# Chunk attention followed by a GELU MLP: GpSimd's casts of later tiles in pieces of 256 elements

## The chip, the cores and the metric

The kernel runs on one core of one Trainium2 chip. Its metric is the device time of one execution in microseconds, as the median over several runs. Besides the times there is one execution taken by the hardware profiler; the profile and the trace that are read below are of that execution. A core has five engines, each with its own queue of instructions: TensorE (PE, with its weight loads shown as PEld), VectorE (DVE), ScalarE (ACT), GpSimd (POOL) and SyncE (SP), which here issues nearly all DMAs. Engines wait for each other through semaphores.

## The reference

```python
def _attn_ref(q, k, v):                       # each (8, 8, 576, 64): batch, heads, sequence, head size
    chunk = 64; nc = S // chunk               # nine chunks of 64 rows
    q_c, k_c, v_c = (a.reshape(B, H, nc, chunk, D) for a in (q, k, v))
    scores = scale * np.matmul(q_c, k_c.transpose(0, 1, 2, 4, 3))
    scores = scores - np.max(scores, axis=-1, keepdims=True)
    attn = np.exp(scores)
    attn = attn / (np.sum(attn, axis=-1, keepdims=True) + 1e-09)
    return np.matmul(attn, v_c).reshape(B, H, S, D)

def _moe_ref(x, w_in, w_out):                 # x (4608, 512), w_in (512, 2048), w_out (2048, 512)
    h = x @ w_in
    g = 0.5 * h * (1.0 + erf(h / sqrt(2)))
    return g @ w_out
```

Attention acts within chunks of 64 rows; its output, with the heads side by side, is the input of a two-layer MLP with the exact GELU.

## The kernel before, in words

**Tiles.** The 4608 rows are worked in nine tiles of 512, numbered 0 to 8. Tiles 0 to 7 are eight chunks of one batch each; tile 8 gathers the ninth chunk of every batch. A tile goes through attention (scores, exponential, sums, product with V) and through the two matmuls of the MLP. While TensorE works on the MLP of tile t, the attention of tile t + 1 and the loads of tiles t + 2 and t + 3 are woven in.

**Saved products.** From tile 1 on both matmuls of the MLP are done in blocks with seven products in place of eight. That takes sums and differences of blocks, which VectorE forms: `x_sums` (line 557) from the attention output, `g_sum` (lines 657 and 670) from the hidden values, `w_in_sums` and `weight_sum` (lines 551 and 522) from the weights. All of these are bf16 subtractions or additions with both inputs in SBUF. The intermediate results of the products are joined by `plus` (line 578), which adds a bank of PSUM and a tile in SBUF and writes either the bank or the tile; TensorE's next product into that bank, at line 574, waits for it. ScalarE copies banks (lines 588 and 591) and applies the GELU (line 582).

**Inputs.** Queries, keys and values arrive as float32 in staging tiles (`arrival`, six of them). `load_qk` (lines 106 to 128) issues one DMA for the queries of a tile and four for its keys, one for each 128 rows; `load_v_rows` issues nine for V of a tile, four for the even heads and five for the odd ones, and sixteen for tile 8. Casts to bf16 follow: `cast_qk` (lines 164 to 171), once for each of four pairs of heads (queries) or of four groups of 128 rows (keys), 512 elements in each partition; and `cast_v_rows` (lines 206 to 210), once for the even and once for the odd heads, 1024 elements each. The function that they are given as `copy` says which engine does it: `PO` is GpSimd, `DV` is VectorE, `AC` is ScalarE. For tiles 2 and later the casts are GpSimd's, but for the keys of tile 2, which VectorE casts. Then `flip` (lines 198 to 204) turns the bf16 queries and keys by a DMA transpose from SyncE's queue, which SyncE issues when the casts are done; `quad_S` multiplies them, and `quad_av` (line 321) reads the cast V as it is.

**Order.** The order of all work is written out by hand. `STEPS` (tiles 2 to 4) and `WHOLE` (tiles 4 to 8) are lists of step names: `CQ`, `CK` and `CV` are the casts of queries, keys and V, `LQ`, `LK`, `LV` the loads, `FQ` and `FK` the flips, `XS1` to `XS4` the `x_sums`, `S1a` to `S4b` the `g_sum`s, `s12` and `c22+` the additions at line 578. In tiles 5 and later the loads and casts stand in `next_loads` (lines 1149 to 1157). Each engine takes its own instructions in this order and waits at an instruction until what it needs is there. `K0` is 2 and `T0` is 3.

Of the kernel before, what the change touches and what calls it, by code (L numbers as in the profile page):

```python
# [11 lines left out]
def kernel(  # L12
# [18 lines left out]
    J = 4  # L31
    PC = CH // J
    G = H // 2
# [3 lines left out]
    CT = NC - 1  # L37
# [126 lines left out]
    def cast_qk(t, nm, g, copy):  # L164
        st = tiles[t]
        if nm not in st:
            st[nm] = ld.tile([P, G, J, 2, D], bf16, tag="k", name="k_nat", bufs=3)
        if nm == "k" and t >= K0:
            copy(st[nm][:, :, g], st[nm + "f"][:, :, g].rearrange("p (q r) d -> p q r d", r=2))  # L169
            return  # L170
        copy(st[nm][:, g].rearrange("p j r d -> p r j d"), st[nm + "f"][:, 2 * g:2 * g + 2])  # L171

# [33 lines left out]
    def cast_v_rows(t, copy):  # L206
        st = tiles[t]
        st["v"] = ld.tile([P, H, CT // 2, D], bf16, tag="v", name="v_nat")
        for r in range(2):
            copy(st["v"][:, r::2], st["vf"][:, r::2])  # L210

    AT, TP, MM = (ps_at, "at"), (ps_tp, "tp"), (ps_mm, "mm")
    ALONE, BETWEEN = (AT, AT, AT, TP), (MM, MM, AT, AT)
# [255 lines left out]
    T0 = 3  # L469
# [181 lines left out]
    def g_sum(t, i, part=None):  # L651

        st = tiles[t]
        n = HF // 2
        if i == 3:
            st["S", 3] = [s3_sb[:, 0:n], s3_sb[:, n:HF]]
            nc.vector.tensor_tensor(s3_sb[:], g_block(t, 0, 0), g_block(t, 1, 0), op=SUB)
            return
        if ("S", i) not in st:
            if i == 4:  # L660
                st["S", i] = [work.tile([P, n, HD], bf16, tag="t1", name="s4", bufs=2)[:] for _ in range(2)]
            else:
                st["S", i] = [flat(k_bds[2 * (i - 1) + a], n) for a in range(2)]
        f = slice(n * part, n * (part + 1))
        a, b, op = {1: (g_block(t, 1, 0), g_block(t, 1, 1), ADD),
                    2: (None, g_block(t, 0, 0), SUB),
                    4: (g_block(t, 0, 1), None, SUB)}[i]
        a = st["S", 1][part] if a is None else a[:, f]
        b = st["S", 2][part] if b is None else b[:, f]
        nc.vector.tensor_tensor(st["S", i][part], a, b, op=op)  # L670
# [113 lines left out]
    def play(t, order):  # L784
# [23 lines left out]
        for m in range(G):  # L808
            does[f"E{m}"] = lambda m=m: quad_exp(n, m)
            does[f"E+{m}"] = lambda m=m: quad_exp(n + 1, m)  # L810
            does[f"ov{m}"] = lambda m=m: quad_over(n, m)
            if t <= T0:
                does[f"R{m}"] = lambda m=m: att_rc(n, m)
                does[f"X{m}"] = lambda m=m: quad_x_plain(n, m)
            else:
                does[f"R{m}"] = lambda m=m: quad_rc(n, m // 2, m % 2)
                does[f"X{m}"] = lambda m=m: quad_x(n, m // 2, m % 2)
            does[f"P{m}"] = lambda m=m: quad_part(n + 1, m // 2, m % 2)
            does[f"XS{m + 1}"] = lambda m=m: x_sums(n, (m,))
            does[f"xs{m + 1}"] = lambda m=m: x_sums(t, (m,))  # L820
            for of in range(4):
                does[f"W{of}.{m}"] = lambda m=m, of=of: w_in_sums(of, (m,))
            does[f"CQ{m}"] = lambda m=m: cast_qk(t + 3, "q", m, PO)
            does[f"CK{m}"] = lambda m=m: cast_qk(t + 3, "k", m, PO)
        does["LQ"], does["LK"] = lambda: load_qk(t + 3, "q"), lambda: load_qk(t + 3, "k")
        does["FQ"], does["FK"] = lambda: flip(n + 1, "q"), lambda: flip(n + 1, "k")
        does["LV"], does["CV"] = lambda: load_v_rows(n + 1), lambda: cast_v_rows(n + 1, PO)
        does["Q8"] = lambda: [load_qk(NT - 1, "q"), pool_cast_qk(NT - 1, "q")]
        for step in order:
# [96 lines left out]
    def pool_cast_qk(t, names="qk"):  # L926
        for nm in names:
            for g in range(G):
                cast_qk(t, nm, g, PO)
# [33 lines left out]
    with tc.manual_schedule():  # L963
# [62 lines left out]
        for c in range(1, NWC):  # L1026
# [8 lines left out]
            if c < 3:  # L1035
                r = slice(CH * (c - 1), CH * c)
# [85 lines left out]
        for t in range(1, NT):  # L1122
            n = t + 1
# [7 lines left out]
            if t == 1:  # L1131
                mm1_slices(1, {0: mm, 1: at, 2: at, 3: mm, 8: mm},
                           (((0, 1, 2), (0,)), last_av, ((0, 1, 2), (1,)), ((3,), (0, 1)), ((8,), (0, 1)),
                            ((0, 1, 2, 3, 8), (2,)), ((0, 3, 8, 1, 2), (3,))))
                x_sums(1)
                for g in range(G):
                    cast_qk(2, "k", g, DV)
                flip(2, "q")
                load_v_rows(2, (0,))
                flip(2, "k")  # L1140
                for ms, y_sb in held:
                    store(0, ms, y_sb)
                held.clear()
                load_v_rows(2, (1,))
                cast_v_rows(2, PO)
                bring_qk(3)
            if t > T0 and n + 1 < NT:
                flip_qk(n + 1)
            def next_loads():
                if t + 3 == NT - 1:  # L1150
                    load_qk(t + 3, "k")
                    pool_cast_qk(t + 3, "k")
                elif t + 3 < NT:
                    bring_qk(t + 3)
                if n + 1 < NT:
                    load_v_rows(n + 1)
                    cast_v_rows(n + 1, PO)
# [7 lines left out]
            g = [[lambda i=i, a=a: g_sum(t, i, a) for i in (1, 2, 4)] for a in range(2)]  # L1165
# [61 lines left out]
```

## Time and profile before

| what | value |
|---|---|
| time, median of 3 runs | 267.56 us (267.51 to 269.14) |
| the profiled execution's own time | 267.8 us |
| its span (first to last instruction) | 266.0 us |
| TensorE clock granted | 1.00 |
| ScalarE busy | 190.7 us, 72% |
| VectorE busy | 223.3 us, 84% |
| GpSimd casts of V, 128x1024 | 14, 1116 ns mean |
| GpSimd casts of keys, 128x512 (line 169) | 24, 671 ns mean |
| GpSimd casts of queries, 128x512 (line 171) | 31, 672 ns mean |
| HBM read and written | 36.70 MB and 9.44 MB |

How to read it: an engine's busy time is the union of its instructions; waiting, branching and the issue of DMAs are not counted. "L574" is line 574 of the kernel. `out<-in` are the program's own tile names, followed by partitions x elements and the type. In the chain of work that ended last, each row is a start, a length and what the time went to; "issue" there is time in which the engine waited for nothing that the profile shows. In a row of the timeline the start and length come first, "x4" is four merged instructions, and square brackets give the engine's idle time before it and what ended that. The ends of matmuls are modelled, so two starts, not one length, tell TensorE's pace. The 31 query casts at line 171 are those of tiles 1 to 8, of which tiles 4 to 8 have 20.

### The profile page before, as it was taken

How to read it: one execution, taken by the hardware profiler on the slowest of the kernel's cores; microseconds unless marked ns; L12 is line 12 of the kernel's file. 1: busy time of each engine (PE TensorE's matmuls, PEld its weight loads, DVE VectorE, ACT ScalarE, POOL GpSimd, SP SyncE). 2: the span in 40 equal slices, each digit the busy share in tenths (PEclk: the TensorE clock that was granted, in tenths of full speed). 3: DMA queues.
4: the chain of work that ended last, by engine and by line, in shares of the span. 5: the costliest groups of instructions: out<-in, count | busy, mean ns of one | idle time of the engine just before them, and what ended most of it. 6: DMA issues, size and time to landing. Idle time of an engine off the chain costs nothing.

```text
span 266.0 us, 7735 instructions
## 1 busy us (share of the span) xinstructions
PE 256.3 (96%) x3121; PEld 210.7 (79%) x3121; DVE 223.3 (84%) x383; ACT 190.7 (72%) x386; POOL 86.1 (32%) x142
## 2 busy tenths in 40 slices
PE   7799999999999999999999998999999999999994
PEld 2478875556888888887878887888888888888883
DVE  6875977989897679678999999999999999947853
ACT  3767758988758988898887587948794789227820
POOL 7768778701267030730540371213200300000000
PEclk9999999999999999999999999999999999999999
DMA  6999998999898989999999988978874220121014
GB/s 209 270 341 402 392 403 210 278 217 276 226 267 206 208 225 276 261 255 234 262 248 193 292 198 215 206 158 192 245 164 90 93 81 2 41 81 41 2 39 118
DMA packets 123412, 53.98 MB, mean 203 GB/s; under 512 B 97776, under 2 KB 120304, under 8 KB 123376
## 3 DMA queue, kind: packets, MB, share of 16 engines
q1 hardware_dynamic: 123072, 53.23, 78.2%
q8 instruction: 24, 0.39, 0.6%
q10 hardware_dynamic: 304, 0.26, 0.3%
q14 instruction: 12, 0.10, 0.1%
HBM read 36.70 MB, written 9.44 MB: 173 GB/s over the span
## 4 chain that ended last, share of the span: by engine, by line
PE 70%; SPq 9%; DMA 6%; ACT 6%; DVE 5%; issue 2%; DVEq 0%
PE hs_ps L574 26%; PE y_ps L734 19%; PE y_ps L764 11%; DMA arrival<-in_moe_w_in_dram 3%; ACT h L582 3%; PE h_ps L438 3%; PE y_ps L897 3%; SPq L123 3%; SPq L162 2%; DMA arrival<-in_k_dram 2%; SPq L117 2%; PE h_ps L454 2%; PE av_ps L321 1%; PE y_ps L861 1%; PE h_ps L464 1%
## 5 line engine op out<-in xcount | busy, mean ns | idle before, releaser
L582 ACT ACTIVATE h<-hs_ps 128x512 bf16<-128x512 f32 x87 | 49.6, 609 | 7.3 <-PE hs_ps L574 6.4
L574 PEld LDWEIGHTS <-w_in_sb 128*128 128x128 bf16 x348 | 33.9, 98 | 4.6 <-issue 0.2
L171 POOL CAST q_nat<-arrival 128x512 bf16<-128x512 f32 x31 | 19.6, 672 | 51.1 <-DMA arrival<-in_q_dram 31.2
L210 POOL CAST v_nat<-arrival 128x1024 bf16<-128x1024 f32 x14 | 15.6, 1116 | 54.0 <-DMA arrival<-in_v_dram 33.5
L574 PE MATMUL hs_ps<-x,w_in_sb 128*128 128x256 bf16 x232 | 31.8, 272 | 0.0
L734 PEld LDWEIGHTS <-h 128*128 128x128 bf16 x240 | 23.2, 98 | 2.8
L961 ACT ACT_TABLE_LOAD x16 | 20.5, 1283 | 1.0 <-PEq L1211 0.7
L694 ACT COPY kept<-y_ps 128x512 f32<-128x512 f32 (+1 forms) x17 | 9.0, 537 | 16.1 <-PE y_ps L734 13.1
L734 PE MATMUL y_ps<-w_out_sb,h 128*128 128x256 bf16 x160 | 18.6, 273 | 0.0
L734 PE MATMUL y_ps<-v_bd,k_bd 128*128 128x256 bf16 x160 | 18.5, 273 | 0.1
L169 POOL CAST k_nat<-arrival 128x512 bf16<-128x512 f32 x24 | 15.4, 671 | 8.2 <-DMA arrival<-in_k_dram 8.1
L734 PEld LDWEIGHTS <-k_bd 128*128 128x128 bf16 x160 | 15.6, 98 | 2.1 <-issue 0.2
L591 ACT COPY hs_ps<-hs_ps 128x512 f32<-128x512 f32 x29 | 16.2, 582 | 0.6 <-PE hs_ps L574 0.5
L574 PE MATMUL hs_ps<-k_bd,w_in_sb 128*128 128x256 bf16 x116 | 16.6, 272 | 0.0
L466 ACT ACTIVATE h<-h_ps 128x512 bf16<-128x512 f32 x21 | 12.5, 605 | 5.3 <-PE h_ps L438 3.9
L244 ACT ACTIVATE pT<-s_ps 128x512 bf16<-128x512 f32 x28 | 14.4, 599 | 1.8 <-PE s_ps L236 1.8
L764 PEld LDWEIGHTS <-h 128*128 128x128 bf16 x144 | 13.8, 98 | 1.7
L699 DVE TENSOR_TENSOR kept<-y_ps,kept 128x512 f32<-128x512 f32 (+1 forms) x16 | 10.4, 649 | 5.4 <-issue 4.0
L574 PE MATMUL hs_ps<-k_bd,w_in_more 128*128 128x256 bf16 x96 | 14.2, 273 | 0.2 <-DVE hs_ps L578 0.2
L574 PEld LDWEIGHTS <-w_in_more 128*128 128x128 bf16 x128 | 12.5, 98 | 2.4 <-issue 0.7
L438 PE MATMUL h_ps<-x,w_in_sb 128*128 128x256 bf16 x128 | 14.3, 273 | 0.1
L438 PEld LDWEIGHTS <-w_in_sb 128*128 128x128 bf16 x128 | 12.3, 98 | 1.9 <-DVE w_in_sb L942 0.4
(158 smaller groups left out, 632.0 us busy)
## 6 DMA issues: line engine op xcount, KB each, us to landing
arrival<-in_v_dram SPq DMA_DIRECT2D x58, 128.0 KB, 3.0
arrival<-in_k_dram SPq DMA_DIRECT2D x28, 256.0 KB, 5.8
arrival<-in_q_dram SPq DMA_DIRECT2D x7, 1024.0 KB, 6.5
out_dram<-kept SPq DMA_DIRECT2D x24, 256.0 KB, 2.8
arrival<-in_moe_w_out_dram SPq DMA_DIRECT2D x4, 1024.0 KB, 12.0
arrival<-in_moe_w_in_dram SPq DMA_DIRECT2D x6, 512.0 KB, 7.9
out_dram<-y_sb SPq DMA_DIRECT2D x8, 256.0 KB, 3.0
arrival<-in_v_dram SPq DMA_DIRECT2D x28, 64.0 KB, 2.6
```

The costliest lines, as they stand in the source:

```text
L169: copy(st[nm][:, :, g], st[nm + "f"][:, :, g].rearrange("p (q r) d -> p q r d", r=2))
L171: copy(st[nm][:, g].rearrange("p j r d -> p r j d"), st[nm + "f"][:, 2 * g:2 * g + 2])
L210: copy(st["v"][:, r::2], st["vf"][:, r::2])
L244: nc.scalar.activation(pT[:].rearrange("p u (c j) -> p u c j", j=J), tiles[t]["s_ps"][m // 2][m % 2][:].rearrange("p u (j c) -> p u c j", ...
L438: nc.tensor.matmul(to[:, cols], left, right[:, cols], start=(start and a == 0), stop=stop, skip_group_check=True)
L466: nc.scalar.activation(tiles[t]["h"][:, f, :], h_ps[:], Act.Gelu)
L574: nc.tensor.matmul(hs[:, f], left[:, ks, f * P:(f + 1) * P], right[:, ks], start=(fresh and f == 0 and ks == 0), stop=(ks == 1), skip_grou ...
L582: nc.scalar.activation(h[:, n:n + HM, HD * c:HD * (c + 1)], src, Act.Gelu)
L591: "s11": lambda: AC(place_of("b")[:], bank["a"][:]),
L734: nc.tensor.matmul(to, left(f, m), right[:, f], start=(fresh and (split or m == 0) and f == 0), stop=(f == HF - 1), skip_group_check=True)
L764: nc.tensor.matmul(bank[name][:, m], left(f, m), right[:, f], start=(fresh and m == 0 and f == 0), stop=(f == HF - 1), skip_group_check=True)
L961: nc.scalar.activation(act_scratch[:], rest[:, 0:1], func)
```

## The change

Three loops are added around copies. Keys of tile 2 and later (the condition is `t >= K0`) are cast in two pieces of two pairs of heads each. Queries of tiles after 3 (`t > T0`) are cast in two pieces, each with two of the four positions `j`. V is cast in four pieces for each half of the heads, one for every 128 rows, wherever `cast_v_rows` is called, which is for tiles 2 to 8. Each piece has 256 elements in each partition where the copy had 512 or 1024. The engine of each cast stays, so the keys of tile 2 are cast in pieces on VectorE. No load, no flip and no other step is moved.

```diff
@@ -166,7 +166,12 @@
         if nm not in st:
             st[nm] = ld.tile([P, G, J, 2, D], bf16, tag="k", name="k_nat", bufs=3)
         if nm == "k" and t >= K0:
-            copy(st[nm][:, :, g], st[nm + "f"][:, :, g].rearrange("p (q r) d -> p q r d", r=2))
+            for q0 in range(0, G, 2):
+                copy(st[nm][:, q0:q0 + 2, g], st[nm + "f"][:, 2 * q0:2 * q0 + 4, g].rearrange("p (q r) d -> p q r d", r=2))
+            return
+        if t > T0:
+            for j in range(0, J, 2):
+                copy(st[nm][:, g, j:j + 2].rearrange("p j r d -> p r j d"), st[nm + "f"][:, 2 * g:2 * g + 2, j:j + 2])
             return
         copy(st[nm][:, g].rearrange("p j r d -> p r j d"), st[nm + "f"][:, 2 * g:2 * g + 2])
@@ -207,7 +212,8 @@
         st = tiles[t]
         st["v"] = ld.tile([P, H, CT // 2, D], bf16, tag="v", name="v_nat")
         for r in range(2):
-            copy(st["v"][:, r::2], st["vf"][:, r::2])
+            for n in range(CT // 2):
+                copy(st["v"][:, r::2, n], st["vf"][:, r::2, n])
```

## The prediction

> **What bounds the kernel now.** I read the page first (busy times, then the chain that ended last), then TensorE's waits after 75 us, then the timeline at the places where TensorE waits. From the page:
>
> ```profile
> span 266.0 us, 7735 instructions
> ...
> PE 256.3 (96%) x3121; PEld 210.7 (79%) x3121; DVE 223.3 (84%) x383; ACT 190.7 (72%) x386; POOL 86.1 (32%) x142
> ...
> PE 70%; SPq 9%; DMA 6%; ACT 6%; DVE 5%; issue 2%; DVEq 0%
> ```
>
> TensorE carries the chain; GpSimd, whose casts are edited, is busy a third of the span and has no share in the chain. So the casts can matter only through something that reaches TensorE. After 75 us TensorE's waits are one line:
>
> ```profile
> PE hs_ps L574 <- DVE hs_ps L578: 1.4, 3, 0.7
> ```
>
> Three waits, all for VectorE's addition at L578. The chain shows them from its own side:
>
> ```profile
> 85.97 0.62 DVE hs_ps L578
> 86.63 4.09 PE hs_ps L574 x36
> ...
> 137.68 0.60 ACT kept_p L588
> 138.27 0.69 DVE hs_ps L578
> ...
> 147.92 0.64 PE av_ps L321 x64
> ...
> 163.37 0.46 issue
> 163.83 0.70 DVE hs_ps L578
> 164.57 8.46 PE hs_ps L574 x76
> ...
> 250.22 12.24 PE y_ps L734 x112
> ```
>
> The last row gives TensorE's pace: 12.24 us over 112 matmuls, 0.109 us each. From 164.57 on it never waits for another engine. Whatever the change saves or costs must pass through three places: near 86, 139 and 164 us.
>
> Why VectorE is late there is seen in the timeline of the first place:
>
> ```profile
> 81.72 2.67 POOL L171 CAST q_nat<-arrival 128x512 bf16<-128x512 f32 x4 [3.77 <-DMA arrival<-in_q_dram]
> ...
> 82.15 0.46 DVE L551 TENSOR_TENSOR arrival<-w_in_sb 128x512 bf16<-128x512 bf16 x1
> ...
> 82.53 0.82 DVE L551 TENSOR_TENSOR arrival<-arrival,w_in_sb 128x512 bf16<-128x512 bf16 x1
> ...
> 83.28 0.68 DVE L578 TENSOR_TENSOR hs_ps<-hs_ps,kept_p 128x512 f32<-128x512 f32 x1
> ...
> 83.88 0.78 DVE L557 TENSOR_TENSOR k_bd<-x,k_bd 128x512 bf16<-128x512 bf16 x1
> ...
> 85.19 0.78 DVE L551 TENSOR_TENSOR arrival<-w_in_sb,arrival 128x512 bf16<-128x512 bf16 x1
> ...
> 85.80 0.60 PE L574 MATMUL hs_ps<-k_bd,w_in_sb 128*128 128x256 bf16 x4
> ```
>
> and of the other two:
>
> ```profile
> 135.93 1.07 POOL L210 CAST v_nat<-arrival 128x1024 bf16<-128x1024 f32 x1 [1.75 <-PE hs_ps L574]
> 136.01 1.26 DVE L557 TENSOR_TENSOR k_bd<-x 128x512 bf16<-128x512 bf16 x1
> ...
> 137.66 0.69 DVE L262 TENSOR_REDUCE part<-pt 128x16 f32<-128x512 bf16 x1
> ...
> 137.91 0.60 PE L574 MATMUL hs_ps<-k_bd,w_in_more 128*128 128x256 bf16 x4
> ```
>
> ```profile
> 151.32 1.10 DVE L670 TENSOR_TENSOR s<-h,k_bd 128x1024 bf16<-128x1024 bf16 x1
> ```
>
> ```profile
> 155.36 0.87 DVE L670 TENSOR_TENSOR s<-h,k_bd 128x1024 bf16<-128x1024 bf16 x1
> 156.16 0.82 DVE L557 TENSOR_TENSOR k_bd<-x 128x512 bf16<-128x512 bf16 x1
> ...
> 157.51 0.41 DVE L557 TENSOR_TENSOR k_bd<-x 128x512 bf16<-128x512 bf16 x1
> ...
> 161.99 0.85 DVE L557 TENSOR_TENSOR k_bd<-x,k_bd 128x512 bf16<-128x512 bf16 x1
> ...
> 163.23 0.69 DVE L262 TENSOR_REDUCE part<-pt 128x16 f32<-128x512 bf16 x1
> ```
>
> ```profile
> 162.81 1.04 PE L574 MATMUL hs_ps<-x,w_in_sb 128*128 128x256 bf16 x8
> ```
>
> The reader is to see one shape with two durations. A bf16 subtraction of 512 elements with both inputs in SBUF takes 0.41 us at 157.51, and 0.78 to 1.26 where it starts inside a GpSimd cast: at 136.01 it starts 0.08 us into the V cast and ends 0.27 after it, so it ran only when the cast let go. The L578 addition, which reads one input from PSUM, takes 0.68 inside casts at 83.28 and 0.70 at 163.83: it isn't held. For the 1024-element form:
>
> ```profile
> L670 DVE TENSOR_TENSOR k_bd<-k_bd,h x16: 679/684/693, 63.3 to 252.7; 128x1024 bf16<-128x1024 bf16 x16
> ```
>
> so 0.68 undisturbed against 1.10 and 0.87 above. VectorE's losses against these bases are: first place 0.05 + 0.41 + 0.37 + 0.37 = 1.20 us; 0.85 ahead of the second; 0.42 + 0.19 + 0.41 + 0.44 = 1.46 between 151 and 163. At the third they cannot drain away, because VectorE has next to no idle time:
>
> ```profile
> 140.00:160.00 20.00, 20.00 (x300) 17.60 (x298) 19.73 (x37) 14.53 (x27) 6.84 (x9) 1.00 1.05 222
> ```
>
> (VectorE 19.73 of 20 us; the last columns are clock, DMA share and GB/s.)
>
> **The change part by part.** *GpSimd's own cost.* No 128x256 cast is in the trace. Its neighbours:
>
> ```profile
> 73.24 2.29 POOL L171 CAST q_nat<-arrival 128x512 bf16<-128x512 f32 x4 [3.26 <-DMA arrival<-in_q_dram]
> ```
>
> ```profile
> 133.56 0.62 POOL L169 CAST k_nat<-arrival 128x512 bf16<-128x512 f32 x1 [0.31 <-DMA arrival<-in_k_dram]
> ```
>
> ```profile
> 138.26 1.04 POOL L210 CAST v_nat<-arrival 128x1024 bf16<-128x1024 f32 x1 [1.27 <-DMA arrival<-in_v_dram]
> 138.69 3.10 SPq L204 DMA_TRANSPOSE q_t<-q_nat  x1
> ```
>
> ```profile
> L176 POOL CAST v_bd<-arrival 64x256 bf16<-64x256 f32 x26 | 10.4, 401 | 1.4
> ```
>
> 512 elements take 0.62, 1024 take 1.04: 0.42 per 512, so 256 take 0.62 - 0.21 = 0.41; the 64x256 row's 0.40 agrees. Four in a row take 2.29, so the next starts (2.29 - 0.62) / 3 = 0.56 after the last, 0.06 before its end; for 256 that spacing is 0.35, for 1024 0.98. Bounds: 0.28 (half of 0.56, no fixed part) and 0.56 (all of it fixed); I take 0.35. By the diff, V of seven tiles goes from 14 casts to 56, keys of tiles 3 to 8 from 24 to 48, queries of tiles 4 to 8 from 20 to 40. GpSimd gains 14 x (1.40 - 0.98) + 44 x (0.70 - 0.56) = 12 us (bounds 2 and 42), some 2 us per tile, against 180 idle us.
>
> *What hides it.* Keys and queries are next read by the flips on SyncE's queue. For tile 6 the last key cast ends at 134.18 and the flip is issued at 138.69: 4.5 us of cover. The last cast starts when its DMA lands and becomes two pieces, 0.14 later; even the eight casts' whole growth, 8 x 0.14 = 1.1, is covered (at the upper bound 8 x 0.56 = 4.5 uses up the cover, and what exceeds it stands in front of SyncE's next loads). V's last cast of tile 5 ends at 139.30 and is read by the attention matmuls at 147.92. Each V piece reads only the rows that one load of the sequence brings, so pieces start as loads land; the last piece ends some 0.6 earlier than now (1.04 - 0.41). No load is brought forward by that: the DMA share is already 1.05.
>
> *VectorE's own casts.* Keys of tile 2 go through the same branch, on VectorE: four casts become eight.
>
> ```profile
> 55.96 0.43 DVE L169 CAST k_nat<-arrival 128x512 bf16<-128x512 f32 x1 [0.22 <-DMA arrival<-in_k_dram]
> ...
> 59.36 0.70 DVE L578 TENSOR_TENSOR hs_ps<-hs_ps,kept_p 128x512 f32<-128x512 f32 x1 [0.70 <-PE hs_ps L574]
> ```
>
> The last waits for its DMA, so only that one's growth counts: between 0 and another 0.43, I take 0.15. It lies under the 0.70 that VectorE then waits for TensorE. Zero on the path.
>
> *VectorE's losses.* A held VectorE instruction waits for the rest of one cast. With pieces the longest rest falls from 0.56 to 0.35 for queries and keys (x 0.63) and from 0.98 to 0.35 for V (x 0.36). First place, all q and k: 1.20 to 0.75, 0.45 saved. Third: (0.42 + 0.19 + 0.41) x 0.63 + 0.44 x 0.36 = 0.80, 0.66 saved.
>
> What of it reaches TensorE: first place, four matmuls from 85.80 last 0.44 at pace, so the next was due at 86.24 and began at 86.63: 0.39 lost, of which 0.45 saved would cover all; I take 0.35, since the new pieces are met at other moments. Second: due 137.91 + 0.44 = 138.35, began 139.00, 0.65 lost; but the chain comes here from ScalarE's copy ending at 138.28 and the 0.69 of L578 follows it. VectorE's own lateness (L262 ends at 138.35) is worth at most 0.1; I take 0.05. Third: due 162.81 + 0.87 = 163.68, began 164.57, 0.89 lost. L578 could have started at 163.37, where the chain shows 0.46 of "issue" under the reduce before it; those 0.46 fall to the 0.66 saved, the rest is the instruction's own time. What is late next there is L578 itself. Sum: 0.35 + 0.05 + 0.46 = 0.86 us.
>
> A rule speaks against the mechanism. The trace first: the casts at 73.24 overlap by 0.06, yet the VectorE instruction at 82.53 ran in between two of the four queued casts. The Trainium skill, "GPSIMD Engine Reference", section "Instruction dispatch", says that consecutive Pool instructions are no barrier, that each of its cores goes on to the next when its own share is done; if so the port need not fall free between two pieces. The same skill's "SBUF — State Buffer", section "Who interferes with whom", has the port held for one whole instruction and then given up. By the first there would be no saving, by the second the 0.86 stands; 82.53 agrees with the second.
>
> **The rivals.** *A: the gain stays hidden.* VectorE is let in earlier, but TensorE's three waits are set by what L578 adds to (second place shows it). Saving 0 to 0.3: 267.3 to 267.6. For: the 138.27 row. Against: "issue" at 163.37.
>
> *B: VectorE loses more.* If a waiting instruction lets more than one piece by, the loss follows GpSimd's total port time instead of one piece's length. It decides from 0.56 / 0.35 = 1.6 pieces per wait on. Port time goes from 14 x 0.98 + 44 x 0.56 = 38.4 to 144 x 0.35 = 50.4, x 1.31. The first place then loses another 0.37, the third 1.46 x 0.31 = 0.45 and, where the 0.85 at 136.01 has not drained, 0.26 more: +1.1 us, 268.6; at the 0.56 bound (80.6, x 2.1) 1.3 + 1.6 + 0.9 = +3.8, 271.4. For: the overlap at 73.24. Against: 82.53 and 155.36, where one cast is let by. The page's rule on Pool instructions is this rival.
>
> *C: more than the sum.* All losses vanish and the three waits go altogether: 0.39 + 0.65 + 0.89 = 1.93, 265.6. It is the ceiling of this mechanism.
>
> *D: the flips are late.* Only near the 0.56 bound; then SyncE's loads slip by a us or so per tile while DMA is full: 269 to 270.
>
> **How the numbers follow.** The profiled execution took 267.8 us, 1.8 beyond its span and 0.24 above the median of 267.56. 267.8 - 0.86 = 266.9 for it; for the median 266.7. Chances: forecast (266.4 to 267.2) 0.55; A 0.18; B 0.13; C 0.08; D and what I don't see 0.06. A measurement of this kernel can tell about 1%, 2.7 us, from no change. Faster by that would need 264.9, beyond the ceiling C: 0.05, for an effect not seen here. Slower by it, over 270.2, needs B near its bound, or D: 0.11. The range leaves out half of C below and the worse half of B and D above: 265.6 to 269.0.
>
> **What would show it.** In the profile after: 128x256 casts of about 0.41 us; L557 and L670 instructions no longer than about 0.41 and 0.68 plus 0.35; the waits of TensorE for L578 at about 0.9 us or less in place of 1.4; flips still issued well after their casts. Forecast wrong: L557 instructions again over 1 us (B), shorter ones with TensorE's waits unchanged (A), casts of over 0.6 us (D), or a new wait of TensorE on another line.

## The result, and the profile after

| | before | after |
|---|---|---|
| median, 20 runs each | 268.08 us (266.61 to 269.55) | 266.69 us (265.30 to 268.05) |
| ratio of the times | 1 | 0.9944, 95% interval 0.9926 to 0.9961 |
| profiled execution, its span | 267.8, 266.0 us | 268.05, 266.3 us |

The change makes the kernel about 1.4 us faster: 0.56%, with an interval that excludes no change. That lies inside the 1% which the prediction called no change, and inside its range; the forecast was 0.86 us, so the sign was right and the size too small. (The median of before has moved from 267.56 with the 17 runs added.)

One thing has to be said before the profile is read: of the 20 executions of after, the profiled one was the slowest, and that of before lay below its median. The two spans don't show the gain. Both kernels were therefore profiled again, before once and after twice (experiments 8 to 10).

The page of after, first execution; in the last three rows the two numbers behind the bar are busy us and mean ns of one:

```profile
PE 256.8 (96%) x3115; PEld 211.8 (80%) x3121; DVE 222.3 (84%) x387; ACT 190.3 (71%) x386; POOL 103.6 (39%) x228
...
PE 76%; ACT 14%; DVE 4%; DMA 3%; issue 1%; POOL 0%; SPq 0%; ACTq 0%; POOLq 0%
...
L216 POOL CAST v_nat<-arrival 128x256 bf16<-128x256 f32 x56 | 24.6, 463 | 38.6 <-DMA arrival<-in_v_dram 38.2
...
L174 POOL CAST q_nat<-arrival 128x256 bf16<-128x256 f32 x40 | 17.6, 488 | 48.3 <-DMA arrival<-in_q_dram 48.3
...
L170 POOL CAST k_nat<-arrival 128x256 bf16<-128x256 f32 x48 | 19.1, 442 | 3.6 <-DMA arrival<-in_k_dram 3.6
```

The pieces are there in the forecast numbers: 56, 40 and 48. GpSimd is busy 17.5 us longer (103.6 against 86.1) and its share of the chain is 0%.

Line numbers behind the casts have grown by 6, so L578 is now L584, L574 is L580, L557 is L563 and L670 is L676. TensorE's waits after 75 us, in the waits view of after (line, what it waited for: us in total, times, longest), in the first and then in the third execution:

```profile
PE y_ps L770 <- ACT kept L777: 0.8, 1, 0.8
PE s_ps L242 <- DMA k_t<-k_nat: 0.6, 1, 0.6
PE hs_ps L580 <- DVE hs_ps L584: 0.2, 1, 0.2
```

```profile
PE y_ps L770 <- ACT kept L777: 0.5, 1, 0.5
PE hs_ps L580 <- DVE hs_ps L584: 0.2, 1, 0.2
```

In the second execution, whose span is 263.7 us, the same view has no row at all. Of the three waits for L578, 1.4 us, there remains one of 0.2 or none. In the first and third executions something else stands in their place, a wait of 0.5 to 0.8 us for `kept` at L777, and in the first also one for the flip of the keys. (Neither needs the pieces: see experiments 8 to 10.) In the chain of the first execution:

```profile
79.00 5.69 PE hs_ps L580 x52
...
96.61 3.59 DMA out_dram<-kept
...
100.27 0.59 ACT kept L777
...
102.81 0.64 PE av_ps L327 x64
...
161.17 12.23 PE hs_ps L580 x112
...
250.49 12.24 PE y_ps L740 x112
```

At the first place TensorE now runs through: 52 matmuls in 5.69 us, 0.109 each. At the third it runs through as well, 112 in 12.23. But at 100.27 ScalarE had to wait for an output DMA of 3.59 us before it could fill `kept` again. The wait for the flip, at 93 us, is one of TensorE that isn't on this chain.

What is nearly the same in every execution of one kernel is the time from the 64 attention matmuls near 101 us to the last 112 matmuls. Here 250.49 - 102.81 = 147.68 us. Before, in its two profiled executions (the last 112 matmuls of the first, at 250.22, are in the prediction):

```profile
101.24 0.64 PE av_ps L321 x64
```

```profile
102.50 0.64 PE av_ps L321 x64
...
251.76 12.24 PE y_ps L734 x112
```

That is 148.98 and 149.26. After, second and third execution:

```profile
100.40 0.64 PE av_ps L327 x64
...
247.93 12.24 PE y_ps L740 x112
```

```profile
101.51 0.64 PE av_ps L327 x64
...
249.24 12.24 PE y_ps L740 x112
```

147.53 and 147.73. In this stretch, which holds the second and third place, the change saves 1.25 to 1.7 us in every pair of executions. Ahead of it the kernels differ by as much between two executions of one kernel (101.24 and 102.50; 100.40 to 102.81) as from each other, and that is where the slow first profile of after lost what it had gained.

VectorE's subtractions, grouped by shape in before and in after (shortest/median/longest ns, from and to us):

```profile
L670 DVE TENSOR_TENSOR k_bd<-h x16: 647/684/1258, 62.5 to 251.9; 128x1024 bf16<-128x1024 bf16 x16
...
L557 DVE TENSOR_TENSOR k_bd<-x x14: 381/417/1275, 78.1 to 235.5; 128x512 bf16<-128x512 bf16 x14
L557 DVE TENSOR_TENSOR k_bd<-x,k_bd x14: 410/415/852, 78.5 to 236.9; 128x512 bf16<-128x512 bf16 x14
```

```profile
L676 DVE TENSOR_TENSOR k_bd<-h x16: 648/688/906, 62.9 to 252.2; 128x1024 bf16<-128x1024 bf16 x16
...
L563 DVE TENSOR_TENSOR k_bd<-x x14: 382/419/699, 78.5 to 235.8; 128x512 bf16<-128x512 bf16 x14
L563 DVE TENSOR_TENSOR k_bd<-x,k_bd x14: 415/476/619, 79.2 to 237.2; 128x512 bf16<-128x512 bf16 x14
```

The last of the three numbers tells the story: the longest waits go from 0.86 us (1275 - 417) to 0.28 (699 - 419). Counted over the trace from 60 us on, with 0.41, 0.68 and 1.22 us as the undisturbed lengths for 512, 1024 and 2048 elements and waits of some 0.05 us and more, VectorE lost 6.6 us in 15 waits before and 3.3, 3.9 and 5.3 us in 20, 24 and 30 waits in the three executions after. A wait now costs 0.16 to 0.18 us on average in place of 0.44, and there are more of them.

### The profile page after: what moved, and what is told of

Its sections match the earlier page's. It is cut to its first block, busy times and chain, and to the rows that moved or that the text cites. A ratio compares the mean times of both kernels' runs of the same rounds, so it can differ in the third digit from the quotient of the medians.

```text
span 266.3 us, 7808 instructions
## 1 busy us (share of the span) xinstructions
PE 256.8 (96%) x3115; PEld 211.8 (80%) x3121; DVE 222.3 (84%) x387; ACT 190.3 (71%) x386; POOL 103.6 (39%) x228
## 3 DMA queue, kind: packets, MB, share of 16 engines
q1 hardware_dynamic: 123072, 53.23, 78.9%
## 4 chain that ended last, share of the span: by engine, by line
PE 76%; ACT 14%; DVE 4%; DMA 3%; issue 1%; POOL 0%; SPq 0%; ACTq 0%; POOLq 0%
PE hs_ps L580 25%; PE y_ps L740 22%; PE y_ps L770 9%; ACT h L588 5%; PE h_ps L444 5%; PE y_ps L903 3%; ACT pT L250 2%; PE av_ps L327 2%; ACT L967 1%; DMA out_dram<-kept 1%; PE y_ps L867 1%; PE h_ps L460 1%; DMA arrival<-in_k_dram 1%; PE tp L187 1%; ACT k_bd L200 1%
## 5 line engine op out<-in xcount | busy, mean ns | idle before, releaser
L216 POOL CAST v_nat<-arrival 128x256 bf16<-128x256 f32 x56 | 24.6, 463 | 38.6 <-DMA arrival<-in_v_dram 38.2
L580 PEld LDWEIGHTS <-w_in_sb 128*128 128x128 bf16 x348 | 33.9, 98 | 4.7 <-issue 0.2
L174 POOL CAST q_nat<-arrival 128x256 bf16<-128x256 f32 x40 | 17.6, 488 | 48.3 <-DMA arrival<-in_q_dram 48.3
L580 PE MATMUL hs_ps<-x,w_in_sb 128*128 128x256 bf16 x232 | 31.8, 272 | 0.0
L170 POOL CAST k_nat<-arrival 128x256 bf16<-128x256 f32 x48 | 19.1, 442 | 3.6 <-DMA arrival<-in_k_dram 3.6
L580 PE MATMUL hs_ps<-k_bd,w_in_sb 128*128 128x256 bf16 x116 | 16.6, 272 | 0.0
L580 PEld LDWEIGHTS <-w_in_more 128*128 128x128 bf16 x128 | 12.5, 98 | 2.3 <-issue 0.5
L580 PE MATMUL hs_ps<-k_bd,w_in_more 128*128 128x256 bf16 x96 | 14.2, 273 | 0.0
```

The source lines that it names most:

```text
L170: copy(st[nm][:, q0:q0 + 2, g], st[nm + "f"][:, 2 * q0:2 * q0 + 4, g].rearrange("p (q r) d -> p q r d", r=2))
L174: copy(st[nm][:, g, j:j + 2].rearrange("p j r d -> p r j d"), st[nm + "f"][:, 2 * g:2 * g + 2, j:j + 2])
L216: copy(st["v"][:, r::2, n], st["vf"][:, r::2, n])
L580: nc.tensor.matmul(hs[:, f], left[:, ks, f * P:(f + 1) * P], right[:, ks], start=(fresh and f == 0 and ks == 0), stop=(ks == 1), skip_grou ...
```

## The experiments

All edits are to the changed kernel unless it is said otherwise; ratios are to the kernel before, on the same chip, with a 95% interval. "Stretch" is the time from the attention matmuls near 101 us to the last 112 matmuls, read from the chain as above.

**1 and 2. One half of the change alone.** First V alone, with the casts of queries and keys as they were; then queries and keys alone, with V as it was.

```diff
-            for q0 in range(0, G, 2):
-                copy(st[nm][:, q0:q0 + 2, g], st[nm + "f"][:, 2 * q0:2 * q0 + 4, g].rearrange("p (q r) d -> p q r d", r=2))
+            copy(st[nm][:, :, g], st[nm + "f"][:, :, g].rearrange("p (q r) d -> p q r d", r=2))
             return
-        if t > T0:
-            for j in range(0, J, 2):
...
```

> V alone in pieces of 256, queries and keys whole as before. Theory (a VectorE subtraction with two SBUF inputs waits for the rest of one GpSimd cast, so the length of a cast is what counts): of TensorE's three waits the first (0.39 us, all queries and keys) stays, the second (0.65) loses about 0.3, the third (0.89) loses about 0.3; 0.6 us less than before, ratio about 0.998. Rival (what helps is that V pieces start as their loads land, a shift in time): all of the change's gain is here, ratio about 0.9945. In the trace the theory expects subtractions of up to 0.8 us beside query and key casts and none over 0.8 beside V casts.

```diff
-            for n in range(CT // 2):
-                copy(st["v"][:, r::2, n], st["vf"][:, r::2, n])
+            copy(st["v"][:, r::2], st["vf"][:, r::2])
```

> Queries and keys alone in pieces of 256, V whole as before. Theory (length of a cast): the first wait goes (0.39), the third shrinks by about 0.4, the second stays; 0.8 us less than before, ratio about 0.997. Rival (V pieces that start with their loads): ratio about 1.000. The theory expects subtractions of 1.2 us beside V casts to remain and those beside query and key casts to stay under 0.65 (512 elements).

V alone: 267.86 us, 0.9972 (0.9940 to 1.0004). Queries and keys alone: 267.31 us, 0.9945 (0.9920 to 0.9970). The gain of queries and keys is clear of no change. For V alone the interval reaches 1 and also holds the rival's 0.9945, so the time decides nothing about V; nor is it shown which half gives more, since the two intervals overlap. The two gains, 0.28% and 0.55%, sum to 0.83%, which the intervals don't tell from 0.56%. VectorE's waits split as they should: beside whole V casts a subtraction of 512 elements still took 1.26 us (0.85 lost), beside pieces of V none lost more than 0.21 us. So did TensorE's losses at the three places, by start times: with V alone 0.28, 0.35 and 0.59 us (in an execution that was the slowest of its twelve), with queries and keys alone none at the first and the third, and 1.16 at the second. The stretch is 149.0 us with V alone and 148.5 with queries and keys alone.

The trace of queries and keys alone held a surprise. Timeline, start and length first:

```profile
132.20 1.80 POOL L170 CAST k_nat<-arrival 128x256 bf16<-128x256 f32 x5
132.51 1.76 DVE L562 TENSOR_TENSOR k_bd<-x,k_bd 128x512 bf16<-128x512 bf16 x1
```

```profile
PE hs_ps L579 <- DVE hs_ps L583: 1.0, 1, 1.0
```

A subtraction of 0.41 us took 1.76. Of the five key pieces in this row, which follow each other without a gap, four lie wholly within it, and TensorE then waited 1.0 us at the second place. This is rival B's mechanism, seen for the first time; it happened to one of 17 held instructions of this execution. Of the 74 in the three executions of the changed kernel none lost more than 0.29 us, less than the 0.345 us from one queued piece to the next.

**3 and 4. Is it the length of a piece, or its earlier start?** A V piece of the change reads only the rows of one load (of two for the last odd piece and in tile 8), so it can start as soon as these have landed; that alone could spread the casts out. Here V is cut by heads instead: pieces of 256 elements again, but each reads all loads of its half of the heads, four or five (in tile 8 eight), so none starts before the last one.

```diff
-            for n in range(CT // 2):
-                copy(st["v"][:, r::2, n], st["vf"][:, r::2, n])
+            for h in range(r, H, 2):
+                copy(st["v"][:, h], st["vf"][:, h])
```

> Queries and keys in pieces as in the change; V in four pieces for each half too, but one for each head, so that every piece needs all loads of its half and none starts early. The pieces are as short (256 elements). Theory (length): the same gain as the change, ratio 0.993 to 0.996. Rival (V pieces that start with their loads): the gain of V is gone, ratio as with queries and keys alone, 0.997 to 1.000.

> V in four pieces by heads, queries and keys as in the change, again. Theory (only the length of a piece counts): the same as the change within 0.002. Its first ratio, 0.991 [0.988, 0.9941], left open that it is better; if that was real it is 0.99 to 0.992 here too and beats the change by 0.7 us or more.

266.19 us, 0.9910 (0.9880 to 0.9941) the first time, and 266.54 us, 0.9939 (0.9917 to 0.9961) with more rounds. The gain is there without the earlier start. The times alone don't settle this for V, because queries and keys alone had 0.9945; the traces add that with V cut by heads no subtraction lost more than 0.25 us in either execution, and the stretch is 148.0 and 147.9 us. For queries and keys an earlier start can't be the cause at all: both pieces of a cast wait for the same loads as the whole cast did, and they gain 0.55% alone. So the length of a piece is what counts. The first run had looked better than the change; the second doesn't tell the two apart.

**5 and 6. Shorter still.** All pieces halved to 128 elements, twice: once timed, once for a second trace.

```diff
-            for q0 in range(0, G, 2):
-                copy(st[nm][:, q0:q0 + 2, g], st[nm + "f"][:, 2 * q0:2 * q0 + 4, g].rearrange("p (q r) d -> p q r d", r=2))
+            for q0 in range(G):
+                copy(st[nm][:, q0, g], st[nm + "f"][:, 2 * q0:2 * q0 + 2, g])
...
-            for j in range(0, J, 2):
-                copy(st[nm][:, g, j:j + 2].rearrange("p j r d -> p r j d"), st[nm + "f"][:, 2 * g:2 * g + 2, j:j + 2])
+            for j in range(J):
+                copy(st[nm][:, g, j], st[nm + "f"][:, 2 * g:2 * g + 2, j])
...
-                copy(st["v"][:, r::2, n], st["vf"][:, r::2, n])
+                for h in (r, r + 4):
+                    copy(st["v"][:, h:h + 3:2, n], st["vf"][:, h:h + 3:2, n])
```

> All the change's pieces halved again, to 128 elements (288 casts). By the two sizes known a piece's spacing is 0.24 us against 0.35. Theory (the rest of one cast): losses fall by another third; of TensorE's waits about 0.34 us was left, so at most 0.1 to 0.2 better than the change: ratio 0.9935 to 0.9945. Rival (loss follows GpSimd's total time at the port, which grows from 50 to 70 us): worse than the change by 0.5 us or more, ratio 0.996 to 0.998; GpSimd is also 3 us later with queries and keys of a tile, which the 4.5 us before the flips should still cover.

> All pieces of 128 once more, for a second trace: the first was of the fastest of its executions. Theory now: waits of VectorE that let several pieces by stand again, in runs of query and key casts, two or more of them, and TensorE waits behind one of them for the addition; the span is 266 us or more. Rival (later flips): TensorE waits for a key or query flip, and no subtraction waits over 0.3 us.

268.84 us, 1.0008 (0.9977 to 1.0039), and 268.22 us in the second look. The theory that a shorter piece is a shorter wait fell here: no gain is left. The rival's 0.996 to 0.998 touches the interval at its upper end only. The first trace, of the fastest of the 12 executions, and the second, the timeline of each:

```profile
110.16 2.04 DVE L564 TENSOR_TENSOR k_bd<-x,k_bd 128x512 bf16<-128x512 bf16 x1
...
110.59 2.00 POOL L170 CAST k_nat<-arrival 128x128 bf16<-128x128 f32 x7
```

```profile
133.69 2.00 DVE L564 TENSOR_TENSOR k_bd<-x,k_bd 128x512 bf16<-128x512 bf16 x1
134.08 2.00 POOL L170 CAST k_nat<-arrival 128x128 bf16<-128x128 f32 x7
```

TensorE's waits after 75 us in the second:

```profile
PE hs_ps L581 <- DVE hs_ps L585: 1.4, 1, 1.4
PE av_ps L328 <- POOL v_nat L217: 0.4, 1, 0.4
```

In each trace one subtraction stood 1.6 us, while six whole pieces went by (the first trace also has a wait of 0.71 us with three and one of 0.31). The waits beside these are as short as the theory wants: the other 27 held instructions of the first trace lost 2.8 us, 0.10 each. So most waits became shorter again and a rare long one took their place. Where it met the second place it cost TensorE 1.4 us; in the first trace it cost 0.5 us near 113 us, and a further 0.4 us lost at 130 us stands under "issue" and isn't explained. The stretch is 148.8 and 149.7 us in the two traces, so nothing of the gain is left there. The second new wait, for a V cast, is the first sight of GpSimd itself being late.

**7. Is it the port time or the run of pieces?** V in pieces of 128, queries and keys in pieces of 256. In experiment 5 up to 32 pieces of queries and keys stood in a row; V's were thought to come in short runs, as their loads land.

```diff
-                copy(st["v"][:, r::2, n], st["vf"][:, r::2, n])
+                for h in (r, r + 4):
+                    copy(st["v"][:, h:h + 3:2, n], st["vf"][:, h:h + 3:2, n])
```

> V in pieces of 128, queries and keys in pieces of 256 as in the change. It tells apart why pieces of 128 throughout gained nothing. In that trace two subtractions let two and six pieces by, both in the long unbroken runs of query and key casts (32 pieces), and waited 0.71 and 1.63 us. Theory now (in a long unbroken run the port is sometimes not handed over at all): V's runs are short, so this is as fast as the change, 0.993 to 0.996. Rival (GpSimd's longer total time at the port costs VectorE more): V's share of it, 56 x 2 x 0.24 = 27 us against 56 x 0.35 = 20, makes it slower than the change by 0.3 us or more, 0.996 to 0.998.

266.32 us, 0.9925 (0.9898 to 0.9953), no wait of TensorE after 75 us, and a stretch of 248.35 - 100.97 = 147.38 us. V in pieces of 128 does no harm, so it is not the added time on GpSimd, 112 casts in place of 56, that costs. What costs in experiments 5 and 6 is in the queries and keys, and the traces show the long waits there; that these make up the whole loss isn't shown. The premise about V was wrong: here its pieces too come up to sixteen in a row (6.72 us from 91.24 on), and yet no subtraction lost more than 0.23 us. So the length of a run alone doesn't decide. In the four longest of these waits, in experiments 2, 5 and 6, the pieces that went by were key casts, but for one query cast in two of them. This variant isn't shown to beat the change: the intervals of the two overlap.

**8 to 10. The same kernels once more.** The kernel before and the changed one were profiled again, and the changed one again with five rounds.

> The kernel before once more, for a second trace. The three waits of TensorE for the addition at line 578 (0.39, 0.65 and 0.89 us by start times) and the long subtractions stand again, 5 to 7 us lost in all after 60 us.

> The changed kernel once more, for a second trace. In the first trace TensorE waited 0.74 us for the key flip of tile 3 and 0.99 us for ScalarE's copy at 100 us. If these come from DMAs that by chance ran late in that execution, one or both are missing here and the span is 264 to 265 us; if they come from the change, they stand here again.

> The changed kernel beside the other runs of this call, on the same chip: ratio 0.993 to 0.996. In its trace no subtraction waits longer than one piece (0.35 us over its base).

Before: 269.38 us. TensorE again waits three times and 1.4 us in all, but not at the same three places. In the waits view and in the chain:

```profile
PE hs_ps L574 <- DVE hs_ps L578: 1.4, 3, 0.6
```

```profile
134.47 10.12 PE hs_ps L574 x92
...
164.30 0.69 DVE hs_ps L578
165.03 8.46 PE hs_ps L574 x76
...
197.46 0.62 DVE hs_ps L578
198.12 2.50 PE hs_ps L574 x20
```

TensorE runs through the second place, with 92 matmuls in 10.12 us, and waits near 198 us instead, where the first execution had no wait. By start times the three waits lose 0.79 (near 87 us), 0.47 and 0.62 us, 1.88 in all, against 1.93 in the first execution. Which casts meet which subtractions changes from one execution to the next, and the places with it; the sum was nearly the same.

After: 265.49 us without any wait, and 266.15 us, 0.9944 (0.9916 to 0.9972), with the two rows shown above. The 1.4 us of before belong to the kernel; the waits for `kept` and the flip come and go. They don't need the pieces. The kernel before, in its second execution, loses 0.25 us to `kept` at 100.59 us, and experiment 11, which has no pieces, waits 0.5 us for `kept` and 0.2 for the flip. They come with late DMAs of tile 3, and why these are late in some executions stayed open: in the first execution of after SyncE issued one key load 1.4 us later than in the first of before (48.70 against 47.34 us), ahead of every changed cast, and the second of before was as late (48.59).

**11. How much is there to win?** The casts of queries, keys and V that the change divides are left out on GpSimd. In the place of each stands a tiny cast and a memset of the whole block, which only writes, so these queries, keys and values are zero.

```diff
+        if nm == "k" and t >= K0 and copy is PO:
+            copy(st[nm][:, 0, g, 0, 0:2], st[nm + "f"][:, 0, g, 0:2])
+            nc.gpsimd.memset(st[nm][:, :, g], 0.0)
+            return
...
-            for j in range(0, J, 2):
-                copy(st[nm][:, g, j:j + 2].rearrange("p j r d -> p r j d"), st[nm + "f"][:, 2 * g:2 * g + 2, j:j + 2])
+            copy(st[nm][:, g, 0, 0, 0:2], st[nm + "f"][:, 2 * g, 0, 0:2])
+            nc.gpsimd.memset(st[nm][:, g], 0.0)
...
+            copy(st["v"][:, r, :, 0:2], st["vf"][:, r, :, 0:2])
+            nc.gpsimd.memset(st["v"][:, r::2], 0.0)
```

> The GpSimd casts of tiles 2 to 8 that the change divides are left out: in their place stands a cast of 2 or 8 elements that waits for the same loads, and one whole memset of the same bf16 tile, so queries, keys and V of those tiles are zero. GpSimd is busy about as long and whole, not in pieces, but reads almost nothing. Theory (a VectorE instruction with two SBUF inputs is held by GpSimd's reading, through a read port that they share): no losses, subtractions of 512 elements at 0.41 to 0.45 throughout; TensorE's three waits go but for about 0.3; ratio 0.993 to 0.994, no worse than the change. Rivals: any GpSimd instruction holds VectorE: subtractions of 0.8 to 1.2 us remain, ratio 0.999 to 1.001; pieces that start early matter: no pieces here, ratio 1.000.

265.97 us, 0.9913 (0.9878 to 0.9949). On the page and in the subtractions by shape:

```profile
L219 POOL MEMSET v_nat<- 128x1024 bf16 x14 | 13.3, 952 | 0.8
```

```profile
L679 DVE TENSOR_TENSOR k_bd<-h x16: 648/683/693, 62.5 to 250.8; 128x1024 bf16<-128x1024 bf16 x16
...
L566 DVE TENSOR_TENSOR k_bd<-x x14: 383/418/426, 78.1 to 234.4; 128x512 bf16<-128x512 bf16 x14
L566 DVE TENSOR_TENSOR k_bd<-x,k_bd x14: 414/416/425, 78.5 to 235.8; 128x512 bf16<-128x512 bf16 x14
```

No subtraction is held at all, though GpSimd works 0.95 us at a time on V. A GpSimd instruction that reads holds these instructions; one that only writes doesn't. It is also the ceiling in the stretch: 249.10 - 101.72 = 147.38 us, 0.15 to 0.35 us below that of the change.

**12. A place further ahead.** In after a VectorE cast of a weight took 1.6 us beside a GpSimd memset of 1.8 us near 23 us. The two memsets of 64x2048 were cut in four.

```diff
-                nc.gpsimd.memset(v_bds[1][r, :, :, o], 0.0)
+                for i in range(0, CT, 2):
+                    nc.gpsimd.memset(v_bds[1][r, i:i + 2, :, o], 0.0)
```

> The change, and the two GpSimd memsets of 64x2048 in the loading phase (1.8 us each, line 1044) in four pieces of 64x512 each. Beside the first of them VectorE's cast of w_in takes 1.62 us in both traces where 0.43 is its undisturbed length, and TensorE's first MLP matmuls follow that cast in the chain. Theory (a cast on VectorE in its faster mode needs GpSimd's port for writing too, and waits for the rest of one instruction): that cast takes 0.9 or less, and up to 1 us of it reaches TensorE: ratio 0.991 to 0.994. Rival (the loads set the pace there): as the change, 0.9945.

266.66 us, 0.9931 (0.9901 to 0.9961). The cast did become shorter, in the timeline of this run:

```profile
22.56 2.18 POOL L1045 MEMSET v_bd<- 64x512 bf16 x4
23.06 0.75 DVE L948 CAST w_in_sb<-arrival 128x512 bf16<-128x512 f32 x1 [0.92 <-DMA arrival<-in_moe_w_in_dram]
```

but the time isn't told from that of the change (0.9944), and the interval holds the theory's 0.991 to 0.994 as well, so a small gain isn't excluded. The trace speaks for the rival, that the loads set the pace: VectorE was waiting for weights before this cast, as the bracket says, and waits 0.57 us for the next load before its cast at 24.39.

## Why the prediction was right, and what was mis-sized

**The mechanism was right.** VectorE's two-input bf16 instructions are held by GpSimd's casts and mostly let in between two of them; shorter pieces make shorter waits (0.44 to 0.17 us on average), and the gain reaches TensorE only where it waits for L578. Experiment 11 shows the hold, experiments 2 to 4 that length and not an earlier start is at work. The signs forecast for the profile came out: no L563 beyond 0.41 + 0.35, and waits for L584 of 0.2 us where 0.9 or less was forecast. Two readings were weaker than they looked. That everything passes through three fixed places held for that one execution; in the second the places were others, with the same sum. And the addition's 0.70 us at 163.83 says nothing about a hold, because no cast runs then; the 0.69 at 138.26, beside a V cast that starts with it, does.

**GpSimd's cost** was right for one piece: an undisturbed piece takes 0.40 us and follows the last after 0.345, against 0.41 and 0.35. The 12 us in all became 17.5 busy us, in part because pieces also wait for VectorE: their mean length is 0.44 to 0.49 us. Both are hidden, as forecast: no V cast was on the chain, and the late flip of the keys at 93 us wasn't GpSimd's: their last piece ended at 78.9 us, and SyncE issued the flip at 88.1. Only pieces of 128 used the cover up (0.4 us in experiment 6). VectorE's own casts of tile 2's keys, put at zero, cost TensorE 0.2 us near 60 us in the first execution and nothing in the other two.

**The third place, forecast 0.46, gave all 0.89 us: this is the term that was mis-sized.** The step that failed is "those 0.46 fall to the 0.66 saved, the rest is the instruction's own time", and with it that L578 itself is late next there. After, in the timeline:

```profile
164.06 1.04 PE L580 MATMUL hs_ps<-x,w_in_sb 128*128 128x256 bf16 x8
164.09 0.69 DVE L584 TENSOR_TENSOR hs_ps<-hs_ps,kept_p 128x512 f32<-128x512 f32 x1
...
164.94 0.60 PE L580 MATMUL hs_ps<-k_bd,w_out_sb 128*128 128x256 bf16 x4
```

The eight matmuls from 164.06 last 8 x 0.109 = 0.87 us at pace, so the next are due at 164.93; they begin at 164.94. The addition starts with the eight and its 0.69 us lie wholly beneath them. Its own time was never on the path; only VectorE's lateness was, and the "issue" of 0.46 in the chain of before was no measure of that. The prediction had the row that says so, its eight matmuls from 162.81, and didn't set the addition beside them. VectorE also gained more than forecast: between 151 and 163 us of before it had lost 1.46 us, and of that 0.51 was left (0.14, 0.20 and 0.17), so 0.95 was saved in place of 0.66. By this count the forecast 0.66 would have left 0.23 of the 0.89 us.

**The second place, forecast 0.05, gave 0.31 us.** In before 0.65 was lost there; after:

```profile
137.45 0.54 DVE L563 TENSOR_TENSOR k_bd<-x,k_bd 128x512 bf16<-128x512 bf16 x1
137.91 0.61 DVE L563 TENSOR_TENSOR k_bd<-x 128x512 bf16<-128x512 bf16 x1
...
139.24 1.07 ACT L594 COPY kept_p<-hs_ps 128x512 f32<-128x512 f32 x2 [0.20 <-PE hs_ps L580]
...
139.48 0.60 PE L580 MATMUL hs_ps<-k_bd,w_in_more 128*128 128x256 bf16 x4
139.51 0.69 DVE L584 TENSOR_TENSOR hs_ps<-hs_ps,arrival 128x512 f32<-128x512 f32 x1
...
140.25 0.60 PE L580 MATMUL hs_ps<-k_bd,w_in_third 128*128 128x256 bf16 x4 [0.18 <-DVE hs_ps L584]
```

Due at 139.48 + 0.44 = 139.92, begun at 140.25: 0.33 lost. The two subtractions lost 0.13 and 0.20 in place of 0.85. The failed step is "VectorE's own lateness (L262 ends at 138.35) is worth at most 0.1", which trusted the chain that came here through ScalarE's copy of `kept_p`. The addition that TensorE waits for reads `arrival`, not `kept_p`, and after it starts at 139.51, in the middle of that copy: it never waited for it. That the copy of before ended as the addition began was chance; what set its start was VectorE's own work ahead of it, which ended with the reduce at L262: before and after, the addition starts 0.09 us ahead of that reduce's end. In the second execution of before no V cast met these subtractions, and nothing was lost at this place.

**The first place, forecast 0.35, gave 0.39 us**, all that was lost there: of VectorE's 1.20 us 0.21 to 0.46 was left in the three executions, where 0.75 was forecast. But what is late next wasn't foreseen: the flip of tile 3 and the store of `kept`, which take it back in some executions. Places together: 1.93 us lost before, 0.33 after in the first execution, 1.60 saved; the ratio 0.9944 gives 0.56% of 268.08, 1.5 us.

**The rivals.** A fell: the stretch is shorter in every execution of the changed kernel than in either of before. B didn't happen in the changed kernel (none of 74 held instructions lost more than one piece's time), and at 82.53 the trace of before had been read rightly; but it is real: more than one piece's time was lost by 1 of 17 in experiment 2 (beside queries and keys), 3 of 30 and 1 of 33 in experiments 5 and 6, and at 128 elements, where the gain is gone, it stands in both traces. What the Trainium skill says in "GPSIMD Engine Reference", section "Instruction dispatch", of consecutive Pool instructions that are no barrier fits these rows (1.76 and 2.00 us for 0.41). The one-instruction hold of the Trainium skill's "SBUF — State Buffer", section "Who interferes with whom", fits the 74. What decides which of the two happens was not found. C, the ceiling of 1.93 us, was nearly reached. D didn't come.

## What to carry to other kernels

When VectorE's SBUF-to-SBUF instructions lose time beside GpSimd's casts, cut the casts, and try more than one size: here 256 elements gave 0.56% and 128 gave nothing, with traces in which a waiting instruction is now and then passed by several small casts. Size what such a cut is worth by setting the late instruction beside the matmuls that run meanwhile, not by the "issue" that the chain shows next to it. Profile a kernel more than once, the one before too, before reading a gain of half a per cent from a trace: the span of one execution had the opposite sign here, and the places where TensorE waits were not the same twice.

## What the runs showed of the hardware that was not expected

GpSimd doesn't always give way between two queued casts. Mostly it lets a waiting VectorE instruction in after one piece, but it also let four pieces of 256 by (1.35 us lost) and six of 128 (1.6 us, twice). Most of these were key casts; V casts in runs of sixteen never did it in experiment 7. A memset on GpSimd, which only writes, doesn't hold VectorE's two-input bf16 subtractions (0.43 us at most for 0.41 in experiment 11), yet it does lengthen a VectorE cast from float32 (1.62 us beside a memset of 64x2048, 0.75 beside pieces of 64x512 in experiment 12). And the cost of a small cast has a large fixed part; queued pieces of 128 elements in experiment 5, in the timeline:

```profile
85.39 3.85 POOL L170 CAST k_nat<-arrival 128x128 bf16<-128x128 f32 x16
```

3.85 us for 16, 0.24 each, against 0.345 for 256 and 0.56 for 512. From these an estimate: about 0.13 us fixed and 0.84 ns for each element in a partition.
